# TensorE's order within one step of an attention loop: the product with v directly behind the scores, then the float32 transposes, then those of k and q

## The chip, the core and the metric

One NeuronCore of a Trainium2 chip runs the whole program as one launch. The metric is device time in microseconds (us). A profiled execution has a span (first to last instruction) and its own device time, which is a little longer.

## What is computed

```python
def _attn_ref(q, k, v):                      # 2 batches, 8 heads, 1152 rows, 64 wide
    q_pool = q.reshape(B, H, S // 2, 2, D).mean(axis=3)          # 576 rows of q per head
    scores = scale * np.matmul(q_pool, k.transpose(0, 1, 3, 2))  # 576 x 1152
    scores = scores - np.max(scores, axis=-1, keepdims=True)
    attn = np.exp(scores)
    attn = attn / (np.sum(attn, axis=-1, keepdims=True) + 1e-09)
    return np.matmul(attn, v)
...
x = attn_out as 1152 x 512
x = _moe_ref(x)      # RMS norm, two products to 1536, silu gate, product back to 512
return _moe2_ref(x)  # product to 2048, mish, product back to 512
```

All of it is kept near float32 accuracy with float16 pairs: a number is split into a high half and the rest (low half), and a product is three float16 products.

## The kernel before

The program has an attention loop of 72 steps (the first 40% of the span), and then the two feed-forward parts, which are bound by TensorE. The change is in the loop.

**Steps and groups.** A group `g` is two heads of one batch; there are 8 groups of 9 steps, n = 0 to 71. A step makes the scores of 128 rows of q against the 1152 columns of k of one head; the step of the group that is left over (number 8 of the group) takes 64 rows of each of its two heads. Below, "step 7" and so on is n modulo 9, and EXP(n), ep(n) name what belongs to the scores of step n.

**The work of one step**, `attn_step(n)`, by engine:

- TensorE: `scores(n)` (L268), six matmuls into three banks of one of two score buffers, the third bank last; in five of nine steps 8 (once 4) float16 transposes of the next group's k and q, `kq_flip` (L205, "flips"); `flip_pe(n - 1)` (L331, "ep"), three float32 transposes of a third of the exponentials of the step before; `attn_v(n - LAG)` (L360 to L363, "AV", LAG is 5), 27 small matmuls of exponentials that are five steps old with v (54 in the step of two heads).
- VectorE: `row_max(n)` (L287, "max"); `kq_keep` (L210, "keep"), which takes the flips out of PSUM; `part_lo(n - 1)` (L141, `et<-ep`, "lo"); after a group of AV products is complete, `attn_r` and `attn_x` (L391 to L408, "r, x"), which divide by the sums; and a scaling of k or v, or the sum of q's pairs.
- ScalarE: `split_hi(n - 1)` (L309, "hl"); `part_hi(n - 1)` (L336, `et<-ep`); in six of nine steps a conversion of k, q or v (L161, L186); `row_exp(n)` (L296, "EXP").
- GpSimd: the low half of the exponentials (L141, `hl`), and SyncE the transposing DMA (L319) of the other two thirds.

**What sets the order.** The whole loop stands under a manual schedule: each engine runs its instructions in the order in which the functions are called, and a step's conversions come from a table (`PLAN`, `FIRST`). The next group's flips are in steps 0, 2, 5, 7 (8 each) and 8 (4) of the group before; the last group has none. The flips of step n are written into the first bank of the score buffer that EXP(n - 1) has just read; the scores of step n + 1 go into the same buffer. So these wait at that bank, which is their third, until keep(n) is done:

```python
        for c in (1, 2, 0):
...
                    if c and n % NTI and kept[n % 2] is not None:

                        tc.declare_no_dep(mm.ins, kept[n % 2].ins, reason="another bank")
```

At step 0 of a group the scores need the new k and q, and wait for the last keep with their first matmul. ep has one buffer: ep(n) waits until lo(n - 1) has read it. AV has one bank per four steps, and its next group waits for x.

Of the kernel before, what the change touches and what calls it, by code (L numbers as in the profile page):

```python
# [28 lines left out]
LAG = 5  # L29
# [11 lines left out]
def kernel(  # L41
# [97 lines left out]
    def lo_op(eng, out_, in_, s, hi):  # L139
        if isinstance(s, float) and s == 1.0:  # L140
            eng.tensor_tensor(out=out_, in0=in_, in1=hi, op=ALU.subtract)  # L141
        else:
            eng.scalar_tensor_tensor(out=out_, in0=in_, scalar=s, in1=hi, op0=ALU.mult, op1=ALU.subtract)
# [50 lines left out]
    def kq_flip(ps_b, g, s0, n):  # L194

        if g not in kqT:
            kqT[g] = kq_p.tile([128, 2 * NJ + 2 * NTI, 128], F16, tag="kqT", name="kqT")
        ps = ps_b.bitcast(F16)[:, 0, :].rearrange("p (s t) -> p s t", s=8)
        for s in range(s0, s0 + n):
            w, z = divmod(s - 2 * NJ, NTI)  # L200
            if s < 2 * NJ:
                src = cvt["k", g][:, s, :]
            else:
                src = cvt["q", g][:, z, w:w + 2, :].rearrange("p t d -> p (t d)")
            nc.tensor.transpose(out=ps[:, s - s0, :], in_=src, identity=ident)  # L205
        flips[g, s0] = (ps, n)

    def kq_keep(z, g, s0):
        ps, n = flips.pop((g, s0))
        kept[z % 2] = nc.vector.tensor_copy(out=kqT[g][:, s0:s0 + n, :], in_=ps[:, 0:n, :])  # L210
# [38 lines left out]
    def where(n):  # L249

        g, j = divmod(n, NTI)
        return g // NP, g, (j if g < NPR - 1 else (j - 1) % NTI)
# [4 lines left out]
    def scores(n):  # L257
        b, g, j = where(n)
        kt = kqT[g][:, 0:2 * NJ, :]
        qt = kqT[g][:, 2 * NJ:, :]  # L260
        ps = s_buf[n % 2]
        heads = [(j % 2, j % 2 * NI + j // 2, 0, 128)] if j < 2 * NI else [
            (e, 2 * NI, e * TL, TL) for e in range(2)]
        per = SN // 128
        for c in (1, 2, 0):
            for e, slot, p0, m in heads:
                for w in range(2):
                    mm = nc.tensor.matmul(  # L268
                        out=ps[p0:p0 + m, c, 0:SN],
                        lhsT=qt[:, w * NTI + slot, p0:p0 + m],  # L270
                        rhs=kt[:, e * NJ + c * per:e * NJ + (c + 1) * per, :].rearrange("p j t -> p (j t)"),
                        start=(w == 0),
                        stop=(w == 1),
                    )
                    if c and n % NTI and kept[n % 2] is not None:

                        tc.declare_no_dep(mm.ins, kept[n % 2].ins, reason="another bank")
        kept[n % 2] = None
        s_t[n] = ps
# [24 lines left out]
    def split_hi(n):  # L304

        if n < 0:
            return
        t = et_p.tile([128, 2, NB * 128], F16, tag="hl", name="hl", bufs=4)
        nc.scalar.activation(out=t[:, 0, :], in_=e_t[n][:, 0:NB * 128], func=ACTF.Copy)  # L309
        hl_t[n] = t  # L310

    def split_lo(n):
        e, t = e_t[n], hl_t[n]
        lo_op(nc.vector if n in LO_DVE else nc.gpsimd, t[:, 1, :], e[:, 0:NB * 128], 1.0, t[:, 0, :])

    def flip(n):
        t = hl_t.pop(n)
        r = et_p.tile([128, 2 * NJ, 128], F16, tag="et", name="et")
        nc.sync.dma_start_transpose(out=r[:, 0:2 * NB], in_=t.rearrange("p w s -> p (w s)"))  # L319
        et_t[n] = r  # L320
# [3 lines left out]
    def flip_pe(n):  # L324

        if n < 0:
            return
        e = e_t[n]
        ps = ps_t.tile([128, PB, 128], F32, tag="t", name="ep")
        for s in range(PB):  # L330
            nc.tensor.transpose(out=ps[:, s, :], in_=e[:, (NB + s) * 128:(NB + s + 1) * 128], identity=idf)  # L331
        ep_t[n] = ps
# [5 lines left out]
    def part_lo(n):  # L338
        if n >= 0:
            r = et_t[n]  # L340
            del e_t[n]
            lo_op(nc.vector, r[:, 2 * NB + PB:, :], ep_t.pop(n), 1.0, r[:, 2 * NB:2 * NB + PB, :])
# [3 lines left out]
    def attn_v(n):  # L346
        b, g, j = where(n)
        et = et_t.pop(n)
        vv = vvt[g]
        if j == x_group(n)[0]:  # L350
            av_t[b] = ps_av.tile([128, 512], F32, tag="av", name="av")
        av = av_t[b]
        heads = [(j % 2, 0, 128)] if j < 2 * NI else [(e, e * TL, TL) for e in range(2)]
        for e, p0, m in heads:
            o0 = (j // 2 % 2 * 2 + e) * (D + 1)
            for jj in range(NJ):
                vr = vv[:, e * NJ + jj, :]
                z = jj if jj < NB else NB + jj
                hi = et[:, z, p0:p0 + m]
                nc.tensor.matmul(out=av[0:m, o0:o0 + D + 1], lhsT=hi, rhs=vr[:, D:2 * D + 1],  # L360
                                 start=(jj == 0), stop=False)
                nc.tensor.matmul(out=av[0:m, o0:o0 + D], lhsT=hi, rhs=vr[:, 0:D], start=False, stop=False)  # L362
                nc.tensor.matmul(out=av[0:m, o0:o0 + D + 1], lhsT=et[:, z + (NB if jj < NB else PB), p0:p0 + m],  # L363
                                 rhs=vr[:, D:2 * D + 1], start=False, stop=(jj == NJ - 1))
# [3 lines left out]
    def x_sums(k=2):  # L368
        for _ in range(min(k, len(sums))):
            rms_sum(*sums.pop(0))  # L370

    def x_group(n):

        b, g, j = where(n)
        if j == 2 * NI:
            return [j]
        k = 2 if g == NPR - 1 and j >= 4 else 4
        return list(range(j // k * k, j // k * k + k))

    def attn_r(n):  # L380
        b, g, j = where(n)
        js = x_group(n)
        if j != js[-1]:
            return
        m = 128 if j < 2 * NI else TL
        i0 = js[0] // 2
        ni = (len(js) + 1) // 2
        o0 = i0 % 2 * 2 * (D + 1)
        a = av_t[b][0:m, o0:o0 + ni * 2 * (D + 1)].rearrange("p (i h c) -> p i h c", i=ni, h=2)
        r = sm_p.tile([128, 2, 2, 1], F32, tag="r", name="r")[0:m, 0:ni]  # L390
        nc.vector.tensor_scalar(out=r, in0=a[:, :, :, D:D + 1], scalar1=eps_sum, scalar2=None, op0=ALU.add)  # L391
        xr[n] = a, r, m, i0, ni
# [3 lines left out]
    def attn_x(n):  # L396
        b, g, j = where(n)
        if n not in xr:
            return
        a, r, m, i0, ni = xr.pop(n)  # L400
        z = i0 // 2
        if (b, z) not in xb2:
            t = xb2[b, z] = xb_p.tile([128, 2 if z < 2 else 1, DM], F32, tag=f"x{z}", name="x")
            for i in range(2 * z, min(2 * z + 2, NI + 1)):
                xb[b, i] = t[:, i - 2 * z, :]
        nc.vector.reciprocal(out=r, in_=r)
        c0 = (g % NP) * 2 * D
        nc.vector.tensor_tensor(  # L408
            out=xb2[b, z][0:m, i0 % 2:i0 % 2 + ni, c0:c0 + 2 * D].rearrange("p i (h d) -> p i h d", h=2),
            in0=a[:, :, :, 0:D], in1=r.to_broadcast([m, ni, 2, D]), op=ALU.mult)  # L410
        if g % NP == NP - 1:
            sums.extend((b, i, m) for i in range(i0, i0 + ni))
# [445 lines left out]
    def each(n, engine):  # L858

        for t, *what in PLAN[engine]:  # L860
            for g in range(1, NPR):
                at = NTI * g + (FIRST[engine].get(t, t) if g == 1 else t)
                if at != n:
                    continue
                if engine == "flip":
                    yield g, FL[what[0]]
                else:
                    f, *a = what
                    f(*([a[0], g, a[1]] if f in (load, kv_hi, kv_lo, kv_scale) else [g, *a]))
# [4 lines left out]

    def attn_step(n):
        scores(n)
        turns = list(each(n, "flip"))
        for g, f in turns:
            kq_flip(read[n - 1], g, *f)
        flip_pe(n - 1)  # L880
        split_hi(n - 1)
        if n:
            split_lo(n - 1)
            flip(n - 1)
        part_hi(n - 1)
        x_sums(1)
        do(n, "act")
        row_max(n)
        for g, f in turns:
            kq_keep(n - 1, g, f[0])  # L890
        part_lo(n - 1)
        row_exp(n)
        do(n, "pool")
        do(n, "load")
        if n >= LAG:
            attn_v(n - LAG)
            attn_r(n - LAG)
            attn_x(n - LAG)
        do(n, "scale")
        read.pop(n - 1, None)  # L900

    with tc.manual_schedule():
# [72 lines left out]
        for step in TAIL:  # L975
# [5 lines left out]
            else:  # L981
                n = NIT - LAG + int(step)
# [116 lines left out]
```

## Time and profile before

| | |
|---|---|
| median of 3 runs | 649.91 us (649.45 to 650.63) |
| the profiled execution | 649.38 us |
| its span | 647.6 us |
| TensorE busy | 586.7 us of the span (91%) |
| VectorE busy | 469.7 us (73%) |
| ScalarE busy | 401.8 us (62%) |
| GpSimd busy | 316.3 us (49%) |

The shares are averages over the loop and the feed-forward parts. In the loop ScalarE and VectorE are busy nine tenths of the time and more; behind it TensorE is, and the other engines fall to a half and less.

### The profile page before, as it was taken

What the parts mean: (1) busy time and instruction counts of PE and PEld (TensorE: products, weight loads), DVE (VectorE), ACT (ScalarE), POOL (GpSimd) and SP (SyncE); (2) the same over time, 40 slices, a digit from 0 to 9 for tenths busy, and PEclk for the clock granted to TensorE, in tenths of its full rate; (3) what the DMA queues carried; (4) which work ended last, traced back from release to release, by engine and by line L of the source; (5) the groups of instructions that cost most, each with busy time, mean ns of one, the idle gap of its engine ahead of it and who ended that gap; (6) DMA issues with size and microseconds to landing.
All of it is one profiled execution on the core that took longest, in us unless ns stands there. A gap on an engine that the chain in (4) does not pass through costs nothing.

```text
span 647.6 us, 16196 instructions
## 1 busy us (share of the span) xinstructions
PE 586.7 (91%) x6600; PEld 479.2 (74%) x6600; DVE 469.7 (73%) x797; ACT 401.8 (62%) x634; POOL 316.3 (49%) x252
## 2 busy tenths in 40 slices
PE   4588988888787788899999999999999999999997
PEld 2366666666565567677777777777888888888986
DVE  4898989989898986668888888476689637264220
ACT  4899999998987886656666664354457415042210
POOL 2787877868786862467777874345430000000000
PEclk9999999999999999999999999999999999999999
DMA  6799999998999997635655664363200000000001
GB/s 198 158 182 204 209 191 199 186 195 173 173 218 215 170 193 151 160 106 188 190 171 171 186 188 155 115 196 131 66 2 1 1 33 2 23 13 2 34 1 50
DMA packets 162075, 84.16 MB, mean 130 GB/s; under 512 B 124752, under 2 KB 152656, under 8 KB 162000
## 3 DMA queue, kind: packets, MB, share of 16 engines
q1 hardware_dynamic: 150896, 66.99, 46.8%
q10 hardware_dynamic: 11104, 16.13, 8.6%
q8 instruction: 52, 0.85, 0.5%
q14 instruction: 23, 0.19, 0.1%
HBM read 50.07 MB, written 2.36 MB: 81 GB/s over the span
## 4 chain that ended last, share of the span: by engine, by line
PE 55%; ACT 16%; DVE 12%; issue 9%; POOL 5%; DMA 1%; ACTq 1%; SPq 0%; DVEq 0%; POOLq 0%
ACT e L296 6%; PE po L778 4%; PE po L779 4%; PE po L777 4%; PE z L585 4%; PE z L586 4%; PE z L587 4%; PE pg L585 3%; PE pg L586 3%; PE pv L587 3%; PE pv L586 3%; PE pv L585 3%; PE pg L587 3%; DVE junk L287 2%; ACT hl L309 2%
## 5 line engine op out<-in xcount | busy, mean ns | idle before, releaser
L141 POOL TENSOR_TENSOR hl<-e,hl 128x768 f16<-128x768 f32 x71 | 118.2, 1667 | 48.8 <-issue 33.9
L287 DVE CUSTOM_DVE_ANT_1 junk<-s,shift 128x1152 bf16<-128x1152 f32 x72 | 97.2, 1351 | 6.9 <-PE s L268 4.9
L296 ACT ACTIVATE e<-s,m 128x1152 f32<-128x1152 f32 x72 | 87.6, 1216 | 14.9 <-DVE m L287 14.5
L268 PE MATMUL s<-kqT 128*128 128x384 f16 (+1 forms) x480 | 83.5, 326 | 10.1 <-DVE kqT L210 8.7
L585 PE MATMUL z<-y,w2i 128*128 128x256 f16 (+1 forms) x320 | 80.5, 262 | 1.2 <-ACT f L731 1.2
L587 PE MATMUL z<-y,w2i 128*128 128x256 f16 (+1 forms) x320 | 80.5, 262 | 0.0
L586 PE MATMUL z<-y,w2i 128*128 128x256 f16 (+1 forms) x320 | 80.5, 262 | 0.0
L360 PE MATMUL av<-vv,et 128*128 128x65 f16 (+1 forms) x720 | 73.6, 193 | 0.9 <-DVE x L408 0.9
L362 PE MATMUL av<-vv,et 128*128 128x64 f16 (+1 forms) x720 | 73.5, 193 | 0.0
L363 PE MATMUL av<-vv,et 128*128 128x65 f16 (+1 forms) x720 | 73.3, 194 | 0.0
L360 PEld LDWEIGHTS <-et 128*128 128x128 f16 (+1 forms) x720 | 67.0, 101 | 2.4 <-issue 2.4
L731 ACT ACTIVATE f<-z 128x512 f32<-128x512 f32 x36 | 21.2, 591 | 74.8 <-PE z L587 74.8
L362 PEld LDWEIGHTS <-et 128*128 128x128 f16 (+1 forms) x720 | 66.7, 99 | 0.7
L450 DVE SCALAR_TENSOR_TENSOR c<-gx,c 128x512 int32<-128x512 int32 x52 | 64.9, 1249 | 3.2 <-ACT gx L434 1.4
L363 PEld LDWEIGHTS <-et 128*128 128x128 f16 (+1 forms) x720 | 66.8, 100 | 0.0
L309 ACT ACTIVATE hl<-e 128x768 f16<-128x768 f32 x72 | 60.7, 843 | 2.7 <-POOL khl L141 0.6
L268 PEld LDWEIGHTS <-kqT 128*128 128x128 f16 (+1 forms) x480 | 38.8, 100 | 31.2 <-issue 11.1
L141 POOL TENSOR_TENSOR h<-fo,h 128x288 f16<-128x288 f32 x48 | 48.5, 1011 | 21.6 <-ACT h L622 21.6
L585 PE MATMUL pg<-stretch 128*128 128x288 f16 x192 | 54.9, 286 | 2.1 <-DMA stretch<-xh 1.6
L434 ACT ACTIVATE gx<-raw 128x512 f32<-128x512 f32 x68 | 45.2, 667 | 17.4 <-issue 9.7
L585 PE MATMUL pv<-stretch 128*128 128x288 f16 x192 | 54.9, 286 | 0.0
L586 PE MATMUL pv<-stretch 128*128 128x288 f16 x192 | 54.9, 286 | 0.0
(127 smaller groups left out, 1697.5 us busy)
## 6 DMA issues: line engine op xcount, KB each, us to landing
raw<-in_moe_w_out_dram SPq DMA_DIRECT2D x28, 512.0 KB, 4.1
raw<-in_moe_w_in_dram SPq DMA_DIRECT2D x16, 512.0 KB, 3.7
raw<-in_moe_w_gate_dram SPq DMA_DIRECT2D x8, 512.0 KB, 3.5
raw<-in_moe_w_val_dram SPq DMA_DIRECT2D x8, 512.0 KB, 3.9
kn<-in_k_dram ACTq DMA_DIRECT2D x14, 288.0 KB, 3.8
vn<-in_v_dram ACTq DMA_DIRECT2D x14, 288.0 KB, 4.3
qn<-in_q_dram ACTq DMA_DIRECT2D x12, 256.0 KB, 3.7
raw<-in_moe_w_gate_dram ACTq DMA_DIRECT2D x4, 512.0 KB, 4.8
```

The costliest lines, as they stand in the source:

```text
L141: eng.tensor_tensor(out=out_, in0=in_, in1=hi, op=ALU.subtract)
L268: mm = nc.tensor.matmul(out=ps[p0:p0 + m, c, 0:SN], lhsT=qt[:, w * NTI + slot, p0:p0 + m], rhs=kt[:, e * NJ + c * per:e * NJ + (c + 1) * p ...
L287: nc.vector.tensor_tensor_reduce(out=junk.rearrange("p (c s) -> p c s", c=SC), in0=ps[:, :, 0:SN], in1=shift.unsqueeze(2).to_broadcast([12 ...
L296: nc.scalar.activation(out=e.rearrange("p (c s) -> p c s", c=SC), in_=ps[:, :, 0:SN], func=ACTF.Exp, bias=m, scale=s_scale)
L309: nc.scalar.activation(out=t[:, 0, :], in_=e_t[n][:, 0:NB * 128], func=ACTF.Copy)
L360: nc.tensor.matmul(out=av[0:m, o0:o0 + D + 1], lhsT=hi, rhs=vr[:, D:2 * D + 1], start=(jj == 0), stop=False)
L362: nc.tensor.matmul(out=av[0:m, o0:o0 + D], lhsT=hi, rhs=vr[:, 0:D], start=False, stop=False)
L363: nc.tensor.matmul(out=av[0:m, o0:o0 + D + 1], lhsT=et[:, z + (NB if jj < NB else PB), p0:p0 + m], rhs=vr[:, D:2 * D + 1], start=False, st ...
L450: nc.vector.scalar_tensor_tensor(out=c, in0=g, scalar=3, in1=c, op0=ALU.logical_shift_left, op1=ALU.bitwise_or)
L585: nc.tensor.matmul(out=ps, lhsT=w0, rhs=x0, start=(i == 0), stop=False)
L586: nc.tensor.matmul(out=ps, lhsT=w0, rhs=x1, start=False, stop=False)
L587: nc.tensor.matmul(out=ps, lhsT=w1, rhs=x0, start=False, stop=(i == n - 1))
```

## The change

In a step, AV is called directly behind the scores, then ep, then the flips; r and x are called behind keep, ahead of lo. Nothing else is changed, and no instruction is added or taken away.

```diff
     def attn_step(n):
         scores(n)
+
+        if n >= LAG:
+            attn_v(n - LAG)
+        flip_pe(n - 1)
         turns = list(each(n, "flip"))
         for g, f in turns:
             kq_flip(read[n - 1], g, *f)
-        flip_pe(n - 1)
         split_hi(n - 1)
         if n:
             split_lo(n - 1)
@@
         row_max(n)
         for g, f in turns:
             kq_keep(n - 1, g, f[0])
+        if n >= LAG:
+            attn_r(n - LAG)
+            attn_x(n - LAG)
         part_lo(n - 1)
         row_exp(n)
         do(n, "pool")
         do(n, "load")
-        if n >= LAG:
-            attn_v(n - LAG)
-            attn_r(n - LAG)
-            attn_x(n - LAG)
         do(n, "scale")
```

TensorE before, at step 17 (the last of the second group), from the last matmul of the scores; `qhl` is the next group's q, `et` the old exponentials, and the semaphore names are those of the engines or of a DMA:

```order
L268 MATMUL s<-kqT 64x384
L205 LDWEIGHTS qhl
L205 MATMUL s<-ident,qhl 128x128 [waits Activation_49]
L205 LDWEIGHTS qhl
L205 MATMUL s<-ident,qhl 128x128
L205 LDWEIGHTS qhl
L205 MATMUL s<-ident,qhl 128x128
L205 LDWEIGHTS qhl
L205 MATMUL s<-ident,qhl 128x128
L331 MATMUL ep<-idf,e 128x128 [waits DVE_49]
L331 MATMUL ep<-idf,e 128x128 x2
L360 LDWEIGHTS et [waits DMAHW6_49]
```

TensorE now, at the same step, first behind the scores and then behind AV's last matmul:

```order
L268 MATMUL s<-kqT 64x384
L360 LDWEIGHTS et [waits DMAHW6_49]
L360 MATMUL av<-vv,et 128x65
L362 LDWEIGHTS et
L362 MATMUL av<-vv,et 128x64
```

```order
L363 MATMUL av<-vv,et 128x65
L331 MATMUL ep<-idf,e 128x128 [waits DVE_49,PE_49,Activation_49]
L331 MATMUL ep<-idf,e 128x128 x2
L205 LDWEIGHTS qhl
L205 MATMUL s<-ident,qhl 128x128
L205 LDWEIGHTS qhl
L205 MATMUL s<-ident,qhl 128x128
L205 LDWEIGHTS qhl
L205 MATMUL s<-ident,qhl 128x128
L205 LDWEIGHTS qhl
L205 MATMUL s<-ident,qhl 128x128
L268 LDWEIGHTS kqT
```

The wait for the exponential (`Activation_49`) stood in front of the flips, with ep and AV behind them; it now stands behind AV, in front of ep, and the next step's scores follow the flips directly. The wait on TensorE itself (`PE_49`) is for an ep of an earlier step.

VectorE at a step 8, the difference; `kqT` is keep, `et<-ep` is lo:

```order
 L210 COPY kqT<-s 128x512 [waits PE_49,Activation_49]
+L391 TENSOR_SCALAR r<-av 128x4
+L406 RECIPROCAL r<-r 128x4 [waits DVE_49]
+L408 TENSOR_TENSOR x<-av,r 128x2x128 [waits DVE_49]
 L141 TENSOR_TENSOR et<-ep,et 128x384 [waits DMAHW4_49,Activation_49]
-L391 TENSOR_SCALAR r<-av 128x4 [waits PE_49]
-L406 RECIPROCAL r<-r 128x4 [waits DVE_49]
-L408 TENSOR_TENSOR x<-av,r 128x2x128 [waits DVE_49]
 L287 ISA junk,m<-s,shift 128x1152 [waits PE_49]
```

r and x stand in front of lo now, in the three steps of a group (3, 4 and 8) in which there is something to divide. ScalarE, GpSimd and SyncE keep their order.

## Rows read from the trace of the kernel before

**Rows 1.** Stretches of the loop: us, busy us of each engine (instructions), clock, DMA share, GB/s
```profile
50.00:75.00 25.00, 22.46 (x358) 16.75 (x355) 22.72 (x46) 23.53 (x31) 20.33 (x15) 1.00 1.07 205
200.00:225.00 25.00, 17.06 (x278) 12.96 (x276) 23.57 (x35) 19.20 (x27) 17.02 (x13) 1.00 0.94 180
```

**Rows 2.** Waits of TensorE, 20 to 300: us in total, times, longest us
```profile
PE ep L331 <- ACT e L296: 14.8, 26, 1.2
PE s L205 <- ACT e L296: 14.3, 16, 2.2
```

**Rows 3.** Waits of ScalarE, 20 to 300
```profile
ACT e L296 <- DVE m L287: 13.6, 15, 2.5
ACT et L336 <- PE ep L331: 6.1, 22, 1.0
```

**Rows 4.** Timeline of ScalarE, steps 6 to 1: start, us, instruction, [idle before <-releaser]
```profile
62.63 1.21 ACT L296 ACTIVATE e<-s,m 128x1152 f32<-128x1152 f32 x1
...
64.88 0.49 ACT L336 ACTIVATE et<-ep 128x384 f16<-128x384 f32 x1 [0.16 <-PE ep L331]
...
68.42 1.21 ACT L296 ACTIVATE e<-s,m 128x1152 f32<-128x1152 f32 x1
...
71.19 1.22 ACT L296 ACTIVATE e<-s,m 128x1152 f32<-128x1152 f32 x1
...
72.45 0.84 ACT L309 ACTIVATE hl<-e 128x768 f16<-128x768 f32 x1
73.20 0.47 ACT L336 ACTIVATE et<-ep 128x384 f16<-128x384 f32 x1
73.57 0.67 ACT L161 ACTIVATE vv<-vn 128x576 f16<-128x576 f32 x1
...
74.14 1.21 ACT L296 ACTIVATE e<-s,m 128x1152 f32<-128x1152 f32 x1
...
89.73 1.21 ACT L296 ACTIVATE e<-s,m 128x1152 f32<-128x1152 f32 x1
```

**Rows 5.** Timeline of TensorE, steps 7 to 2
```profile
63.90 0.61 PE L205 MATMUL s<-ident,qhl 128*128 128x128 f16 x8 [0.59 <-ACT e L296]
64.34 0.50 PE L331 MATMUL ep<-idf,e 128*128 128x128 f32 x3
...
68.56 1.14 PE L268 MATMUL s<-kqT 128*128 128x384 f16 x6 [0.32 <-DVE kqT L210]
...
70.12 0.50 PE L331 MATMUL ep<-idf,e 128*128 128x128 f32 x3
...
72.47 0.55 PE L331 MATMUL ep<-idf,e 128*128 128x128 f32 x3
72.85 0.19 PE L360 MATMUL av<-vv,et 128*128 128x65 f16 x1
...
73.68 1.14 PE L268 MATMUL s<-kqT 128*128 128x384 f16 x6
```

**Rows 6.** Timeline of VectorE, steps 7 to 0
```profile
64.62 0.69 DVE L210 COPY kqT<-s 128x1024 f16<-128x1024 f16 x1
...
65.88 0.95 DVE L148 TENSOR_SCALAR kn<-kn 128x576 f32<-128x576 f32 x1
66.81 1.36 DVE L287 CUSTOM_DVE_ANT_1 junk<-s,shift 128x1152 bf16<-128x1152 f32 x1
...
68.09 0.42 DVE L210 COPY kqT<-s 128x512 f16<-128x512 f16 x1
68.42 0.55 DVE L141 TENSOR_TENSOR et<-ep,et 128x384 f16<-128x384 f32 x1
68.89 0.15 DVE L391 TENSOR_SCALAR r<-av 128x4 f32<-128x4 f32 x1
...
69.73 1.36 DVE L287 CUSTOM_DVE_ANT_1 junk<-s,shift 128x1152 bf16<-128x1152 f32 x1
```

**Rows 7.** Timeline of ScalarE in the first group, step 4
```profile
28.44 0.49 ACT L336 ACTIVATE et<-ep 128x384 f16<-128x384 f32 x1 [1.01 <-PE ep L331]
```

## The prediction

> **What bounds the kernel now.** I read the stretches first, then what TensorE and ScalarE wait for, then the timeline of one round of nine steps. In a stretch in the middle of the loop ScalarE is busy 23.5 of 25 us, VectorE 22.7 and TensorE 22.5 [rows 1]: no engine has much room, and ScalarE has the least. Later, where the norm's work is mixed in, VectorE is the fullest (23.6 of 25) and TensorE has room (17.1). The granted clock is 1.00 in both, the 2.4 GHz level, so it is no part of this. TensorE waits for an exponential 42 times, 29.1 us in all [rows 2]: this is the hole that AV could fill. But what counts is what ScalarE waits for: 13.6 us for a maximum, and 6.1 us in 22 places for ep [rows 3]. One round takes 27.10 us, from EXP(6) at 62.63 to the next at 89.73 [rows 4].
>
> **The costs that the replay uses** are distances between starts. ScalarE: from EXP to hl 1.26 (71.19 to 72.45), hl to part_hi at the earliest 0.75, part_hi to what follows 0.37, a conversion to EXP 0.57 (73.57 to 74.14) [rows 4]; a step is then 2.38, or 2.95 with a conversion, if nothing is waited for. part_hi can't start before ep's start + 0.54 (64.34 to 64.88) [rows 4, 5]. TensorE: AV 0.83 (72.85 to 73.68), ep 0.38 (72.47 to 72.85), eight flips 0.44 (63.90 to 64.34), their data complete after 0.61; the scores 1.12, the row's 1.14 less the overlap with what follows [rows 5]. VectorE: max 1.28 (66.81 to 68.09), keep 0.69, of four flips 0.42, lo 0.47, r and x 0.84 (68.89 to 69.73), the scaling of k 0.93 [rows 6].
>
> **The change, part by part.** No instruction is added, so all of it is order. AV moves in front of ep and of the flips, ep in front of the flips.
>
> *Where TensorE is early*, AV fills the wait and costs nothing, and ep, now first behind the wait, comes 0.44 sooner than behind eight flips. *Where TensorE is late*, AV's 0.83 stands between the scores and ep, and ep sits on ScalarE's path: hl takes 0.75 after EXP, and any ep that starts later than 0.75 + 1.26 - 0.54 = 1.47 after EXP's start delays part_hi and the next EXP one for one. What makes TensorE late is the flips: they now end directly before the next scores, so keep, which had AV, ep and four score matmuls (2 us) as cover, has the four matmuls alone (two thirds of 1.12, 0.75), and keep itself starts 0.4 to 0.5 later, behind ep.
>
> Replayed from the same start (EXP(6) at 62.63, scores of step 7 done at 63.28):
>
> Step 7: AV to 64.11, ep 64.11 to 64.49, flips to 64.93. part_hi 64.65, EXP(7) 65.03; before, part_hi was at 64.88 [rows 4], so 0.23 is won. keep starts at 65.12, not 64.62 [rows 6], and ends at 65.81; lo and the scaling to 67.13.
>
> Step 8: the third bank waits for keep, scores to 66.24, AV to 67.07, ep 67.07, part_hi 67.61, EXP(8) 68.55 against 68.42. max to 68.41, keep to 68.83, r and x to about 69.6.
>
> Step 0: all its scores wait for keep, from 68.88 (before 68.56 [rows 5]) to 70.00; AV to 70.83, ep 70.83 against 70.12; part_hi 71.37, EXP(0) 71.75 against 71.19. The flips run to 71.65, keep to 72.53.
>
> Step 1: scores to 72.96, again held at the third bank; AV to 73.79, ep 73.79 against 72.47 [rows 5]; part_hi 74.33 against 73.20, EXP(1) 75.27 against 74.14 [rows 4]: 1.13 lost in four steps.
>
> Carried through steps 2 to 6 in the same way it stays near that (0.98 to 1.76, since step 4 has an AV of twice the length), and the round ends 1.17 late. A second round starts better, since TensorE then enters it 1.35 ahead of EXP(6) and not 0.47: I get EXP(1) 0.9 late, and 0.94 for the round. I take 0.94, with 1.17 as the other end.
>
> r and x in front of lo: 0.84 in three steps of nine. lo's reader on TensorE is the next ep, which waits for lo to free its buffer; in the replay lo(7) ends at 70.07 and ep(8) starts at 70.83, so it costs nothing. The cover is the late ep itself: were ep(8) ready at EXP(8)'s end, 69.76, this would cost 0.3 a round.
>
> The DMAs: AV now starts up to 1.9 us earlier in its step (0.44 + 0.38 and a wait of up to a microsecond are no longer ahead of it). What it reads was sent in the step four before, three full steps of some 2.95 ago, and TensorE's list of waits shows none on such a transfer, so I cost this at nothing.
>
> The start: in step 4 of the first group part_hi waits 1.01 for ep [rows 7], since ep stands behind flips that wait for GpSimd's half of k. ep goes ahead of them, and 0.6 of this should be left when the next steps are through (bounds 0 and 1.1).
>
> The sum: the four rounds from EXP(6) at n = 6 to n = 42 at 0.94 make +3.8. In the 20 steps after that VectorE often sets the pace [rows 1], where a late ep costs less; between nothing and the full 20/9 x 0.94 = 2.1 I take half, +1.0. The last nine steps have no flips: TensorE needs 0.38 + 1.12 + 0.83 = 2.33 a step there, and ep comes in time, so nothing. With -0.6 at the start that is +4.2. Behind the loop TensorE is the bound and starts later by as much. The profiled execution took 649.38, so 653.6; the median of the runs is 0.5 above it, so 654.1. Bounds of this case: 4 x 0.94 - 1.1 = +2.7 and 4 x 1.17 + 2.1 = +6.8, that is 652.6 to 656.7.
>
> *A rule weighed.* The rows say: TensorE waits 29.1 us for exponentials [rows 2], but ScalarE can give back no more than the 6.1 us for which it waited on TensorE [rows 3]. The Trainium skill, Perfetto Trace Analysis, section Optimization Strategies (under Optimizing DMA Performance), says that the goal in general is to keep the matmul engine as highly used as possible. By that rule the filled waits would be worth up to 29.1 us, an estimate of 649.9 - 29.1 = 620.8; by the rows ScalarE's path decides, and the sum above stands. The rule in its mild form is the first rival.
>
> **Rivals.**
>
> *Faster: TensorE stays early.* If AV is over before the exponential in nearly every step, ep comes first behind the wait, and ScalarE's 6.1 us for ep go [rows 3]: 643.8 at best, 646 if two thirds go. For it: 42 of 72 steps have TensorE waiting, 0.69 on average, nearly AV's 0.83. Against it: the steps in which ScalarE waits for ep are those with flips, where TensorE is not early, and the next scores are held by keep. The point from which it decides is whether ep can start within 1.47 of EXP's start; the replay misses this by 0.7 at step 0 (70.83 against 68.55 + 1.47 = 70.02).
>
> *No change.* ScalarE and VectorE have 23 of 25 us of work of their own [rows 1]. If what step 7 gains and the start gives equals what the late steps lose, or if VectorE's order absorbs it, the time stays at 649.9, give or take 1.
>
> *Slower, by more.* The upper bound, +6.8, and on top VectorE, which now idles some 0.4 before each keep in the 35 steps with flips, 14 us; where it is the fullest engine a fifth of that, 2.8, would reach the end: 659.5.
>
> **How the numbers follow.** About 0.2% (1.3 us) is what a measurement of this kernel can tell from no change. My forecast has 0.56, faster 0.19, no change 0.15, slower by more 0.10. 0.03 of the forecast is a loss under 1.3 us, and 0.01 of the no-change case a gain over it. So slower by over 0.2% is 0.10 + 0.53 = 0.63, within 0.2% 0.14 + 0.03 = 0.17, faster 0.19 + 0.01 = 0.20. The forecast's own range is 652 to 657. To hold 8 in 10 it reaches down to 647, which takes in the no-change case and the mild end of the faster one, and up to 657.5. The predicted time is 654.1.
>
> **What would show it.** Right: ScalarE's waits for ep grow from 6.1 us to 15 or more, in the steps 8, 0, 1, 3 and 4; a round is 28.0 us and not 27.1; TensorE's waits for exponentials shrink, and it waits for keep in most steps behind flips. Each keep starts 0.4 or so later against EXP. Wrong: if waits for ep fall below 6 us, TensorE stayed early; if a round is unchanged but the time is longer, the loss is in the later 20 steps or behind the loop; if AV waits for a transfer, its data came too late.

## The result, and the profile after

The changed kernel took 658.85 us (median of 4 runs, 658.17 to 660.18), the kernel before 649.79 beside it (649.45 to 650.63): a ratio of 1.0146, 95% interval 1.013 to 1.0163. It is slower, as forecast, but by 9.06 us and not by 4.2. The profiled execution took 658.34 us.

The head of its page: span, busy time with its share, and the granted clock in 40 slices.

```profile
span 656.6 us, 16231 instructions
...
PE 593.2 (90%) x6600; PEld 486.9 (74%) x6600; DVE 471.1 (72%) x797; ACT 401.6 (61%) x634; POOL 315.1 (48%) x252
...
PEclk9999999999999898899999999999999999999999
```

The same row of the page of before:

```profile
PE 586.7 (91%) x6600; PEld 479.2 (74%) x6600; DVE 469.7 (73%) x797; ACT 401.8 (62%) x634; POOL 316.3 (49%) x252
```

TensorE has 6600 matmuls in both, and yet it is busy 6.5 us longer. That fits the row of the clock, which is below 9 in three of its 40 slices where the page of before has 9 in all: some of its work ran at a lower clock.

Waits of the changed kernel, 20 to 310 us: us in total, times, longest.

```profile
PE ep L331 <- ACT e L296: 23.7, 27, 3.0
PE s L268 <- DVE kqT L210: 16.6, 29, 2.1
ACT et L336 <- PE ep L331: 14.6, 32, 1.3
ACT e L296 <- DVE m L287: 9.9, 12, 2.4
...
PE pg L585 <- DMA stretch<-xh: 3.0, 1, 3.0
```

Two of them in the kernel before:

```profile
PE s L268 <- DVE kqT L210: 8.7, 10, 2.7
...
PE pg L585 <- DMA stretch<-xh: 1.6, 1, 1.6
```

TensorE waits 23.7 us for exponentials where it waited 29.1 [rows 2]; its hole did get smaller. ScalarE's wait for ep grew from 6.1 to 14.6, its wait for a maximum fell from 13.6 to 9.9 [rows 3], and the scores wait for keep in 29 places for 16.6 us, where it was 10 places and 8.7 us.

The same round on ScalarE's timeline, EXP of steps 6 to 6, with part_hi's waits left out:

```profile
64.08 1.21 ACT L296 ACTIVATE e<-s,m 128x1152 f32<-128x1152 f32 x1
66.44 1.21 ACT L296 ACTIVATE e<-s,m 128x1152 f32<-128x1152 f32 x1
69.99 1.21 ACT L296 ACTIVATE e<-s,m 128x1152 f32<-128x1152 f32 x1
72.66 1.22 ACT L296 ACTIVATE e<-s,m 128x1152 f32<-128x1152 f32 x1
76.79 1.22 ACT L296 ACTIVATE e<-s,m 128x1152 f32<-128x1152 f32 x1 [0.48 <-DVE m L287]
...
91.91 1.21 ACT L296 ACTIVATE e<-s,m 128x1152 f32<-128x1152 f32 x1
```

The round takes 27.83 us, where it took 27.10 [rows 4]. The starts of one instruction in both traces, subtracted, show where the whole time went:

| place (before's time for the last five) | after less before, us |
|---|---|
| EXP(4), EXP(6) | -1.01, -0.23 |
| EXP(15), (24), (33), (42) | +1.45, +2.18, +2.79, +3.77 |
| EXP(62) | +3.84 |
| EXP(63), EXP(71), the last | +4.50, +4.96 |
| first gate of the feed-forward part (L613, 251) | +4.95 |
| L613 at 258 | +6.60 |
| L613 at 273 | +6.58 |
| L613 at 275 | +8.29 |
| L613 at 278, and from there on | +8.93 |

So 5.0 us are lost in the loop and 4.0 behind it, in two jumps. Here are those two places, and the two stretches of [rows 1], in the changed kernel: us, busy of PE, PEld, DVE, ACT, POOL, clock, DMA share, GB/s.

```profile
50.00:75.00 25.00, 22.21 (x360) 17.50 (x361) 22.33 (x43) 23.07 (x31) 19.44 (x14) 1.00 1.06 205
200.00:225.00 25.00, 20.56 (x321) 16.21 (x318) 22.01 (x41) 20.89 (x29) 17.96 (x13) 0.93 1.07 201
...
250.00:255.00 5.00, 4.88 (x27) 3.40 (x28) 2.73 (x5) 4.25 (x10) 1.16 (x1) 0.66 1.10 297
270.00:275.00 5.00, 3.59 (x17) 2.30 (x18) 3.45 (x7) 4.78 (x9) 1.83 (x2) 0.66 0.44 81
```

The clock is 0.66 in both places, that is 1.2 GHz for part of the stretch and 2.4 for the rest. The same two places in the kernel before, where it is 1.00:

```profile
245.00:250.00 5.00, 4.84 (x60) 4.11 (x61) 2.74 (x5) 4.27 (x10) 1.16 (x1) 1.00 0.99 258
263.00:268.00 5.00, 4.06 (x32) 3.13 (x33) 3.44 (x7) 4.36 (x8) 1.42 (x2) 1.00 0.36 66
```

TensorE's timeline of the changed kernel shows what came ahead of each:

```profile
248.07 0.19 PE L363 MATMUL av<-vv,et 128*128 128x65 f16 x1
250.12 0.55 PE L331 MATMUL ep<-idf,e 128*128 128x128 f32 x3 [1.86 <-ACT e L296]
250.51 0.29 PE L585 MATMUL pg<-stretch 128*128 128x288 f16 x1
...
250.88 0.45 PE L585 MATMUL pg<-stretch 128*128 128x288 f16 x1
```

```profile
271.41 0.42 PE L585 MATMUL pg<-stretch 128*128 128x288 f16 x1 [3.00 <-DMA stretch<-xh]
271.62 0.45 PE L586 MATMUL pg<-stretch 128*128 128x288 f16 x1
```

Behind the first wait the same matmul starts every 0.12 us at first (250.51 and two more until 250.88), and then 14 times every 0.24; behind the second it starts 14 times every 0.21 to 0.24 at once. Each stretch so costs 1.6 to 1.7 us of TensorE's time. At the loop's end the idle time is the change's own doing. Before, the last AV products stood behind ep(70), and TensorE then waited 1.05 us for EXP(71):

```profile
245.16 0.55 PE L331 MATMUL ep<-idf,e 128*128 128x128 f32 x3 [1.05 <-ACT e L296]
```

Now part of them is done ahead of ep(70), so less is left to fill the last wait: 1.86 us.

That TensorE bounds the stretch behind the loop stands, but the other engines do not all fall to a half there: on the page of before VectorE is at eight tenths in seven slices running.

### The profile page after: what moved, and what is told of

Same layout as the page of the kernel before. It is cut to its first block, busy times and chain, and to the rows that moved or that the text cites. A ratio compares the mean times of both kernels' runs of the same rounds, so it can differ in the third digit from the quotient of the medians.

```text
span 656.6 us, 16231 instructions
## 1 busy us (share of the span) xinstructions
PE 593.2 (90%) x6600; PEld 486.9 (74%) x6600; DVE 471.1 (72%) x797; ACT 401.6 (61%) x634; POOL 315.1 (48%) x252
## 4 chain that ended last, share of the span: by engine, by line
PE 60%; ACT 12%; DVE 12%; issue 8%; POOL 3%; DMA 3%; ACTq 1%; SPq 0%; DVEq 0%; POOLq 0%
PE po L777 4%; PE po L778 4%; PE po L779 4%; PE z L585 4%; PE z L587 4%; PE z L586 4%; ACT e L296 4%; PE pg L585 4%; PE pg L587 4%; PE pg L586 4%; PE pv L585 4%; PE pv L586 4%; PE pv L587 4%; DVE junk L287 3%; DMA qn<-in_q_dram 2%
## 5 line engine op out<-in xcount | busy, mean ns | idle before, releaser
L268 PE MATMUL s<-kqT 128*128 128x384 f16 (+1 forms) x480 | 88.5, 331 | 18.0 <-DVE kqT L210 16.6
L360 PE MATMUL av<-vv,et 128*128 128x65 f16 (+1 forms) x720 | 74.6, 194 | 2.9 <-DVE x L408 2.2
L268 PEld LDWEIGHTS <-kqT 128*128 128x128 f16 (+1 forms) x480 | 42.4, 101 | 43.8 <-issue 25.1
L363 PE MATMUL av<-vv,et 128*128 128x65 f16 (+1 forms) x720 | 74.4, 195 | 0.0
L331 PE MATMUL ep<-idf,e 128*128 128x128 f32 x216 | 38.8, 289 | 27.0 <-ACT e L296 25.1
L585 PE MATMUL pg<-stretch 128*128 128x288 f16 x192 | 56.0, 292 | 3.0 <-DMA stretch<-xh 3.0
L587 PE MATMUL pg<-stretch 128*128 128x288 f16 x192 | 56.1, 292 | 0.0
L586 PE MATMUL pg<-stretch 128*128 128x288 f16 x192 | 56.0, 292 | 0.0
```

The source lines that it names most:

```text
L268: mm = nc.tensor.matmul(out=ps[p0:p0 + m, c, 0:SN], lhsT=qt[:, w * NTI + slot, p0:p0 + m], rhs=kt[:, e * NJ + c * per:e * NJ + (c + 1) * p ...
L585: nc.tensor.matmul(out=ps, lhsT=w0, rhs=x0, start=(i == 0), stop=False)
L586: nc.tensor.matmul(out=ps, lhsT=w0, rhs=x1, start=False, stop=False)
L587: nc.tensor.matmul(out=ps, lhsT=w1, rhs=x0, start=False, stop=(i == n - 1))
```

## The experiments

The theory: in the loop AV's place loses the time, and behind it TensorE's half clock does. The rivals: the order of ep and the flips, the last nine steps, the place of r and x, and a cause behind the loop that has nothing to do with the clock. All compare with the kernel before on the same chip (medians of 649.16 to 649.53 us). Some profiles have EXP(0) already 0.6 to 0.9 us later than in the trace of before, ahead of anything that an edit touches; the offsets below that carry it say so.

### Which of the two moves costs the loop

Only ep in front of the flips; AV, r and x at the end of the step, as before (the diff is against the kernel before):

```diff
         turns = list(each(n, "flip"))
+        flip_pe(n - 1)
         for g, f in turns:
             kq_flip(read[n - 1], g, *f)
-        flip_pe(n - 1)
```

> Only ep is moved in front of the flips; AV, r and x stay where they were before the change. Theory A (AV between the scores and ep makes ScalarE wait, and TensorE idle before it drops to half clock): neither happens here, keep has AV as cover again; within 1 us of before, or up to 2 us faster since ep no longer stands behind flips that wait for GpSimd in the first group; about 649, clock 1.00 throughout the loop. Rival B (the loss comes from ep in front of the flips, since keep and so the next scores' third bank come 0.4 us later): some 3 to 5 us slower than before, with waits of the scores for keep as in the changed kernel (about 17 us).

Measured: 649.81 us, ratio 1.0009 (0.9993 to 1.0025). The loop ended 2.34 us sooner than before, and all of it was given back behind the loop. Its waits, and then one of two stretches at a lower clock behind the transfer of xh:

```profile
PE ep L331 <- ACT e L296: 28.1, 42, 2.2
...
PE pg L585 <- DMA stretch<-xh: 3.2, 1, 3.2
...
ACT et L336 <- PE ep L331: 1.2, 5, 0.2
```

```profile
264.00:266.00 2.00, 2.00 (x10) 1.26 (x9) 1.20 (x3) 1.99 (x6) 0.77 (x2) 0.51 1.05 195
```

ScalarE's wait for ep is all but gone (1.2 of 6.1 [rows 3]): this half of the change is good for the loop. Of the 2.34, 0.9 is there at EXP(42). Another 1.4 comes at EXP(59), where one VectorE instruction of the norm took 2.13 us in the trace of before, with GpSimd busy beside it throughout, and 0.74 in this one, with GpSimd mostly idle:

```profile
200.49 2.13 DVE L546 SCALAR_TENSOR_TENSOR xn<-x,w,gbc 128x512 f32<-128x512 f32 x1
```

```profile
199.53 0.74 DVE L546 SCALAR_TENSOR_TENSOR xn<-x,w,gbc 128x512 f32<-128x512 f32 x1
```

That is not the move's doing: in the run below with the order of before up to step 62 it took 0.74, and in the two later runs with ep alone in front 2.20 and 2.13. So the move is worth 0.9 us in the loop.

The other half, AV with r and x in front, and ep left behind the flips (against the changed kernel):

```diff
-        flip_pe(n - 1)
         turns = list(each(n, "flip"))
         for g, f in turns:
             kq_flip(read[n - 1], g, *f)
+        flip_pe(n - 1)
```

> Only AV (with r and x) is moved, directly behind the scores; then flips, then ep, as before. Theory A: ScalarE's waits for ep grow beyond the 14.6 us of the changed kernel, since ep now stands behind AV and the flips, and TensorE idles before the exponentials as in the changed kernel, so the clock falls too: 656 to 662. Rival B: most of the loss is gone, about 651, and waits for keep are near those of before (9 us).

Measured: 653.15 us, ratio 1.0056 (1.0038 to 1.0074); the loop ended 3.63 later (0.75 of it there at EXP(0)), and nothing was added behind it.

```profile
PE s L268 <- DVE kqT L210: 16.3, 16, 2.1
...
ACT et L336 <- PE ep L331: 13.2, 35, 1.1
```

Both waits are near those of the changed kernel. Up to EXP(42), counted from EXP(0), AV alone in front loses 4.14 us, the whole change 3.65, and ep alone gains 0.90: the loss of the four rounds is AV's place. At EXP(71) it is 2.88 against 4.84; where the change lost the rest, behind EXP(50), is only in part known (0.66 of it is told below). The time lies in neither range, and the clock did not fall behind the loop, as theory A had said, though the last wait for an exponential is 1.87 us here too.

### Loop or last nine steps

The changed order up to step 62 and the old one in the last nine, and the reverse (`n >= 63`); r and x go with AV (against the kernel before, in part):

```diff
+        new = n < 63
+        if new:
+            if n >= LAG:
+                attn_v(n - LAG)
+            flip_pe(n - 1)
+            for g, f in turns:
+                kq_flip(read[n - 1], g, *f)
+        else:
+            for g, f in turns:
+                kq_flip(read[n - 1], g, *f)
+            flip_pe(n - 1)
...
+        if not new:
+            if n >= LAG:
+                attn_v(n - LAG)
```

> The changed order in steps 0 to 62, the order of before in the last nine, which have no flips. Theory C (4 of the 9 us come from two stretches at half clock behind the loop, and the first of them from TensorE's longer idle time at the loop's end, 1.86 us against 1.05): the stretch at half clock at the loop's end is gone, and 1.6 to 4 us of the 9 with it: 655 to 657.5. Rival D (the clock's fall has nothing to do with the order at the loop's end, or costs nothing): 658 to 659, or only the 0.5 us that the last nine steps lost.

> The order of before in steps 0 to 62, the changed order in the last nine. Theory C: TensorE idles longer before the last exponential, the clock falls there as in the changed kernel, and 1.6 us (4, if the second stretch at half clock comes too) are lost behind the loop, beside some 0.5 in the steps: 651.5 to 654.5. Rival D: 650 to 650.5, clock 1.00 throughout.

Measured: 656.31 us, 1.0106 (1.0089 to 1.0123), and 651.28 us, 1.0025 (1.0011 to 1.0039). So the last nine steps, with what they bring on behind them, are worth 1.8 to 2.3 us of the 9 (651.28 - 649.53, and 9.06 less 656.31 - 649.53). The first time is in theory C's range, the second just below it and above rival D's.

Both traces are of executions faster than the median (654.04 and 649.61). In the first the last wait for an exponential is 1.05 us again, the loop ends 3.81 later, the clock is 1.00 behind it, and the time grows to +4.62 at a wait for xh of 3.1 us. In the second the last wait is that of the changed kernel, and still the clock does not fall, and nothing is added behind the loop:

```profile
245.42 0.55 PE L331 MATMUL ep<-idf,e 128*128 128x128 f32 x3 [1.87 <-ACT e L296]
```

```profile
245.00:250.00 5.00, 4.58 (x58) 3.90 (x59) 2.79 (x6) 4.27 (x10) 1.16 (x1) 1.00 1.01 285
```

So the longer wait does not by itself bring the half clock: of the five traces here whose last wait is 1.86 or 1.87 us, it fell behind it in the changed kernel alone. The ten times of this kernel fall into two groups, 649.45 to 650.83 us (five, mean clock 0.991 to 0.997) and 651.74 to 653.49 (five, 0.987 to 0.992). That fits a clock that falls there in some executions and not in others, but only one of the ten has a trace.

### Is it the half clock

The changed kernel with idle float32 transposes of the identity (their result is overwritten) where TensorE waits: 16 ahead of ep in step 56, 11 ahead of the last ep, 12 at the wait for xh. Then the same without the last 12. (In part, against the changed kernel.)

```diff
+FILL = {55: 16, 71: 11}
...
+        for s in range(FILL.get(n, 0)):
+            nc.tensor.transpose(out=ps[:, 0, :], in_=idf, identity=idf)
         for s in range(PB):
```

> The changed kernel with work added that nothing reads: 16 float32 transposes of the identity ahead of ep in step 56, 11 ahead of the last ep at the loop's end, and 12 where TensorE waits for the norm's transposed rows behind the loop, each in a place where TensorE idled 1.9 to 3.0 us. Theory C (stretches at half clock behind such idle time cost 1.6 us at the loop's end and about 1 us at the later wait): the time falls to 655.5 to 657.5, and the granted clock stays at 1.00 behind the loop. Rival D (the half-clock stretches cost nothing, and the 4 us behind the loop are transfers or other waits): 658 to 659.5, or more by the added work.

> The changed kernel with idle transposes only at the loop's end (16 in front of ep in step 56, 11 in front of the last ep), none at the wait for xh. With all three fills it was 655.4. Theory C (each stretch at half the granted clock behind the loop costs time of its own): the half clock at the loop's end stays away, that behind the wait for xh may come, so the offset grows by 0 to 0.5 us up to 273 us and by 0.5 to 2.5 us behind it: 655.5 to 658. Theory D (the clock has nothing to do with it; the gain of the fills came from something at the wait for xh): as the changed kernel, 658 to 660.

Measured: 655.40 us, 1.0089 (1.0075 to 1.0102), and 655.06 us, 1.0079 (1.0065 to 1.0093), against 658.85 without: both just under theory C's range. Added work made the kernel faster; against the kernel before beside each it is 6.0 and 5.6 us slower and not 9.1. The two stretches, with the fills at the loop's end alone:

```profile
250.00:255.00 5.00, 5.00 (x65) 4.32 (x64) 2.73 (x5) 4.26 (x10) 1.16 (x1) 1.00 1.04 274
270.00:275.00 5.00, 4.47 (x37) 3.43 (x36) 3.63 (x6) 4.20 (x9) 3.15 (x3) 1.00 0.67 117
```

The clock is 1.00 in both. The offset is +4.96 at EXP(71), as in the changed kernel (0.72 of it there at EXP(0)), and then +5.27 to the end, not +8.93. The wait for xh is 1.6 us and not 3.0 without any fill there; why the transfer landed 1.4 later in the changed kernel was not tested. A wait of about 3 us stands in five of the twelve traces without a fill at that place, with AV last in the last steps too (ep alone in front, 3.2; the old order in the last nine, 3.1), so the half clock at the loop's end is not its cause in all of them. In the latter the clock stays at 1.00 behind it, and 0.81 us is lost there:

```profile
268.72 0.30 PE L585 MATMUL pg<-stretch 128*128 128x288 f16 x1 [3.09 <-DMA stretch<-xh]
```

```profile
268.00:273.00 5.00, 4.28 (x35) 3.44 (x36) 3.47 (x5) 4.49 (x9) 2.62 (x3) 1.00 0.58 107
```

The changed kernel lost 2.35 there (8.93 - 6.58). The fills in step 56 and at the last ep were not tried one by one.

The same on the two other orders:

> The kernel before with 6 added transposes at the loop's end and 12 at the later wait. Theory C: before, the clock seldom falls at these places with a cost, so at most 0.5 us is won: 648.8 to 649.6, with less spread. Rival D: 649.5 or a little more.

> Only ep moved in front of the flips (AV, r, x where they were before the change), with the same kind of added work: 12 transposes ahead of ep in step 56, 6 at the loop's end, 12 at the later wait. Theory C: the loop keeps its gain of 2.3 us over before, and what was lost behind the loop is not: 646.5 to 648.5, faster than before. Rival D: 649.5 to 650.5, no better than without the added work.

Measured: on the order of before (6 at the loop's end, 12 at xh) 650.61 us, 1.0015 (1.0006 to 1.0025): slower, where theory C had a gain. The trace of before has no half clock at these places to save, and 12 transposes outlast a wait of 1.6 us; the offset grows by 0.97 at that place. On ep alone in front (12, 6 and 12) 649.0 us, 0.9988 (0.9977 to 1.0), half a microsecond short of what theory C expected, which counted on 2.3 us from the loop.

### r and x behind lo

The changed kernel, with r and x moved behind lo:

```diff
+        part_lo(n - 1)
         if n >= LAG:
             attn_r(n - LAG)
             attn_x(n - LAG)
-        part_lo(n - 1)
```

> The changed kernel, but r and x behind lo, as their order to lo was before the change. Theory A (r and x in front of lo cost nothing, since ep is late anyway): 658 to 660. Rival E (r and x in front of lo hold up lo, the EXP behind it or the next AV): 655 to 657.

Measured: 666.27 us, 1.0249 (1.0225 to 1.0273). Neither theory had this. TensorE's wait for x is 16.1 us, where it is 2.2 in the changed kernel:

```profile
PE av L360 <- DVE x L408: 16.1, 20, 2.1
```

One such place on TensorE, and ScalarE behind it:

```profile
84.65 0.19 PE L360 MATMUL av<-vv,et 128*64 128x65 f16 x1 [1.03 <-DVE x L408]
```

```profile
87.03 0.49 ACT L336 ACTIVATE et<-ep 128x384 f16<-128x384 f32 x1 [1.30 <-PE ep L331]
```

AV's bank is free only when x has read it. With AV in front of ep, a late x delays ep too.

### AV in the middle

Two more places for AV, with r and x ahead of lo: ep, AV, flips (the diff, against the changed kernel), and flips, AV, ep.

```diff
+        flip_pe(n - 1)
         if n >= LAG:
             attn_v(n - LAG)
-        flip_pe(n - 1)
         turns = list(each(n, "flip"))
```

> TensorE's order in a step: scores, ep, AV, flips; r and x in front of lo as in the changed kernel. Theory A (the loop is lost because AV stands in front of ep, so that ScalarE's part_hi waits): ScalarE's wait for ep in the stretch from 20 to 310 us falls from 14.6 us to under 3, the loop ends at most 1 us later than before, and the time is 649 to 651. Theory K (the loop is lost because AV stands in front of the flips, so that keep and with it the next scores come late): the wait of the scores for keep stays near 16 us (16.6 in the changed kernel, 16.3 with only AV in front), the loop ends 3 us or more later than before, and the time is 653 to 656.

> TensorE's order in a step: scores, flips, AV, ep; r and x in front of lo. Theory A: ep has AV in front of it in every step, ScalarE's wait for ep is 13 us or more as with the changed order, the loop ends 3 us or more later, time 653 to 657. Theory K: the flips stand where they stood before, so the wait of the scores for keep is near the 8.7 us of before, the loop ends within 1 us of before, time 649 to 651.

Measured: 661.83 us, 1.0184 (1.0169 to 1.02), and 670.82 us, 1.0331 (1.0303 to 1.0359); the loops ended 12.31 and 21.05 later (0.77 of the second there at EXP(0)). Both theories fell as alternatives: in direction each holds in one of the two, and both times are above either's range. With ep, AV, flips ScalarE's wait for ep is 11.6 us, where theory A had under 3, and the wait of the scores for keep 13.5, where theory K had 16. With AV ahead of the flips alone VectorE stands waiting for them, and the maximum behind keep comes late:

```profile
DVE kqT L210 <- PE s L205: 18.6, 22, 2.1
ACT e L296 <- DVE m L287: 17.9, 26, 2.4
```

With AV ahead of ep alone ScalarE waits:

```profile
ACT et L336 <- PE ep L331: 35.2, 41, 1.6
```

My reading of these waits, which no run takes apart: an AV in the middle stands behind what waits for EXP (ep, or the flips, whose bank EXP reads). It can't use that wait, and all of its 0.83 delays whoever stands behind. In front it can, and the changed kernel loses least of the three.

That left open whether r and x ahead of lo were the price in these two. Only their place changed in the next two: ahead of lo with AV last, and behind lo with ep, AV, flips.

> TensorE's order in a step: scores, ep, flips, AV as with ep alone in front (649.8); r and x in front of lo. Theory V (r and x in front of lo are dear wherever AV is not in front, since VectorE then stands at r until AV is done, and lo and the next maximum wait behind it): VectorE's wait for AV at r is 10 us or more (4.3 before), time 654 to 664. Theory F (AV's place on TensorE alone decides; r and x cost nothing): as with ep alone in front, 649 to 651.

> TensorE's order in a step: scores, ep, AV, flips, which gave 661.8 with r and x in front of lo; here r and x stand behind lo as in the kernel before. Theory V: the wait at r falls from 9.8 us to under 5 and the time to 650 to 656. Theory F (AV ahead of the flips makes keep and so the next scores late): VectorE's wait for the flips stays near 18.6 us, time 659 to 664.

Measured: 650.09 us, 1.0009 (0.9998 to 1.0019), and 662.32 us, 1.0201 (1.0179 to 1.0224), against 649.81 and 661.83 with the other place. VectorE's wait at r rose to 10.6 us in the first, as theory V has it, but it reached no end; TensorE's order decides. r and x matter only where AV is in front and waits for x.

### A version that keeps the gain

ep alone in front of the flips, and 12 idle transposes at the wait for xh (the diff shows these alone):

```diff
+        for s in range(12):
+            nc.tensor.transpose(out=ps[:, 0, :], in_=idf, identity=idf)
         fill += [(0, 2), (1, 2)] + [(f, c) for f in range(2, NWB) for c in range(3)]
```

> Only ep moved in front of the flips, and 12 idle transposes at the wait for xh, none within the loop. With ep alone in front the loop ended 2.34 us sooner and the wait for xh with a half-clock stretch gave 2.6 us back. Theory C: the loop's gain is kept, 647 to 648.5, below before. Theory D: the wait for xh is a transfer's and the fill changes nothing, 649.5 to 650.5, no gain.

Measured: 648.89 us (11 runs) against 649.46 (15 runs), ratio 0.9986 (0.9977 to 0.9994). It has the lowest median of all kernels here, by less than the 0.2% named in the prediction, though its interval lies below 1. Its profile has a mean clock of 1.00 and a wait for xh of

```profile
PE pg L585 <- DMA stretch<-xh: 0.7, 1, 0.7
```

Its loop ends 0.09 sooner than before, from a start that was 0.80 later; nothing is given back behind it. It fell 0.4 short of the upper end that theory C gave.

## Why the prediction was right and wrong

**Right: the direction and the mechanism in the loop.** "AV's 0.83 stands between the scores and ep, and ep sits on ScalarE's path" is what the runs show: ep alone in front is a gain of 0.9 in the loop, AV in front a loss. ScalarE's wait for ep was to grow "to 15 or more" and is 14.6, and 13.0 of it lies in the steps that the prediction named, 8, 0, 1, 3 and 4. A round was to be 28.0 and is 27.83. The four rounds cost 3.77 + 0.23 = 4.00, against +3.8, but singly 1.68, 0.73, 0.61 and 0.98.

**Partly luck: the replay's times.** It had EXP(8) 5.92 behind EXP(6), and the rows above give 69.99 - 64.08 = 5.91. EXP(0) was to come 9.12 behind and came 8.58, as early as before (71.19 - 62.63 = 8.56 [rows 4]). EXP(1) was to come 12.64 behind and came 12.71, but 0.48 of that is a wait for a maximum, which the replay did not have: VectorE's scaling of v took 1.56 us there, and 0.52 in the trace of before. The late ep alone would have brought EXP(1) at about 12.2.

**Right: the rule that was weighed.** The Trainium skill (Perfetto Trace Analysis, Optimization Strategies) has it as the goal in general to keep the matmul engine as highly used as possible. Read as the prediction reads it, filling TensorE's waits should have paid. Its waits for exponentials fell by 29.1 - 23.7 = 5.4 us, and the time rose by 9. ScalarE's wait was the one that counted in the loop. Behind the loop, where TensorE is the bound, idle time did cost: the wait for xh was 1.4 us longer, and 2.35 was lost there.

**Mis-sized, nearly cancelling: three terms of the loop.** The start is -0.23 and not -0.6 (bounds 0 and -1.1). The 20 steps up to EXP(62) cost +0.07 where +1.0 stood. EXP(58) was 6.96 late, and 3.1 of it was back by EXP(59); 1.4 of this is the instruction xn again, 0.74 here and 2.13 in the trace of before, so a trace of before with the short one would have given about +1.5. The last nine cost +1.12 where "nothing" stood. 0.66 of that is half clock: in step 63 the scores waited 2.07 for keep, and AV and ep ran at the lower clock behind them (ep 0.88 us, not the 0.50 of [rows 5]), so that part_hi waited 0.71 for ep. 0.49 is AV in front, which waits 1.34 us for x at step 68:

```profile
221.49 0.88 PE L331 MATMUL ep<-idf,e 128*128 128x128 f32 x3
222.17 1.82 PE L268 MATMUL s<-kqT 128*128 128x384 f16 x6
...
236.40 0.19 PE L360 MATMUL av<-vv,et 128*64 128x65 f16 x1 [1.34 <-DVE x L408]
```

Together the loop is +4.96 for a forecast of +4.2, well inside the bounds.

**Wrong: "Behind the loop TensorE is the bound and starts later by as much."** It lost 3.97 more there, and that alone put the time out of the range. By the offsets it is 1.6 of half clock at the loop's end and 2.35 at the wait for xh: some 0.8 of this is the later landing (what the old order in the last nine lost by it at a clock of 1.00), and 1.5 is half clock. The error began in the first paragraph: the clock was 1.00 in two stretches [rows 1], "so it is no part of this". That was read from one execution of the kernel before (the mean clock of its others goes from 0.986 to 1.00), and carried over to an order that moves TensorE's idle time. The prediction moved AV out of the last wait for an exponential and never asked what was left in it. With that wait filled both jumps are gone: 0.31 is added behind the loop and not 3.97. What stays open is why the clock falls behind that wait in this trace and not in four others with the same wait, and why xh landed late.

**"r and x in front of lo ... costs nothing"** held, in the sense that their place alone moves nothing while AV comes last. What the text did not see is that in this change they are needed there: without them it is 7.4 us slower.

**The rivals.** The faster one (TensorE stays early) failed where the text placed the doubt, in the steps with flips. The upper case of 659.5 comes near in number, but its mechanism, VectorE idle before each keep, is not what reached the end: the 20 steps where it should have cost +0.07.

## What to carry to other kernels

Work that fills one engine's wait is free only if the next thing on that engine is not what a fuller engine waits for: put the instruction that feeds the bound first, and the filler last. When an order changes, look at the idle time that the moved work used to cover, above all at the seam into a stretch that TensorE bounds, since a wait there can be followed by some microseconds at 1.2 GHz. Take a granted clock of 1.00 as a reading of one execution of the old order, not as a property of the program.

## What the hardware did that I had not expected

Idle time of 1.86 us was followed by half clock at the loop's end, worth 1.6 us. But idle time alone does not decide it. The kernel before waited longer within the loop, with the clock at 1.00:

```profile
204.55 0.48 PE L268 MATMUL s<-kqT 128*128 128x384 f16 x2 [2.66 <-DVE kqT L210]
```

Nor does the order decide it. The scores of step 63, in the kernel before and in the one with the old order up to step 62: TensorE has had the same instructions until there, the wait is the same, and the scores take 1.17 us in the first (clock 1.00 from 214 to 217 us) and 2.13 in the second (0.59 from 213 to 216).

```profile
215.12 1.17 PE L268 MATMUL s<-kqT 128*64 128x384 f16 x12 [1.86 <-DVE kqT L210]
```

```profile
213.75 2.13 PE L268 MATMUL s<-kqT 128*64 128x384 f16 x12 [1.86 <-DVE kqT L210]
```

Nor does the mean clock of a run tell its time: runs of the kernel before beside the experiments took 648.30 to 651.13 us with 0.986 to 0.989, and 648.06 to 650.68 with 1.00. In the loop, where TensorE has room, the stretches at 1.2 GHz at step 63 cost 0.66 us in the changed kernel and 1.16 in the run above; behind it each one is paid in full. Idle transposes of the identity were enough to hold 1.00 through both places here.
